# Attention into a feed-forward layer on one core: a planner that counts the early matmuls, the fillers and the V loads differently

## The chip, the core and the metric

The kernel runs on one core of one Trainium2 chip. The metric is device time in microseconds (us) of one execution; lower is better. The engines are TensorE (PE in the profile; PEld is its weight load), VectorE (DVE), ScalarE (ACT), GpSimd (POOL) and SyncE (SP). Each works through its own list of instructions in order and waits on semaphores for the others.

## The reference

Block-causal attention over 8 batches of 8 heads, 576 positions of 64 numbers, in blocks of 64; its output, as 4608 rows of 512, goes through a two-layer network of width 2048.

```python
def _attn_ref(q, k, v):                      # 8, 8, 576, 64
    scores = np.matmul(q, k.transpose(0, 1, 3, 2)) / np.sqrt(D)
    mask = (pos // 64)[:, None] >= (pos // 64)[None, :]
    scores = np.where(mask, scores, -1e9)
    attn = softmax(scores)
    return np.matmul(attn, v)

def _moe_ref(x, w_in, w_out, beta):          # x 4608 x 512, w_in 512 x 2048, w_out 2048 x 512
    h = x @ w_in
    g = h * (1.0 / (1.0 + np.exp(-beta * h)))
    return g @ w_out
```

## The kernel before

Nothing in this kernel is ordered by hand. The program first writes down every piece of work as an `Op` of a class `Plan`: the engines that may do it, how long it holds its engine (`dur`), when its result is there (`lat`), what it depends on, which buffers it takes, a priority, and for a transfer the time that it takes on the queue (`xfer`). `Plan.schedule` then plays all of it through on the host: whenever an engine is free in this play, it takes the op of the lowest priority number whose inputs are there. What comes out of it is one list of ops for each engine. These lists, with the semaphore waits that they need, are the kernel. The planned times themselves do not reach the chip; only the order does, and the count of the fillers described below.

**The work.** A unit is two heads of one batch, so there are 32 units, `u`, four to a batch `b`. For each unit:

- q and k are loaded by SP (L608 for batches 0 and 1, L642 from batch 2 on), cast to bf16 (`QKn`; L615, L653; nearly always on POOL), and turned, so that the head dimension lies on the partitions (`QKT`). In batches 0 and 1 PE turns them (L624) and DVE copies them out (L632); from batch 2 on SP issues a transposing transfer for each pair of units (L660).
- PE multiplies q by k (L692, L436) into PSUM, ACT takes the exponential (L706, L718) into `E`, DVE zeroes the masked corners (L712, L714).
- v is loaded by SP into `Vs` (L538, L541), one such tile for each batch in six transfers, and cast to `Vn` by POOL (L564). In batch 0 the loads for heads 4 to 7 go partly by POOL's queue straight into `Vn`.
- PE multiplies `E` by `Vn` (L744, 30 matmuls of 65 columns), DVE divides by the sum (`inv` L756, `xq` L763). The result is turned into `xT`, by PE for batches 0 to 2 (L783, copied out by L791 and L793), by SP's transposing transfer from batch 3 on (L770).

The network then runs over chunks of 512 rows, `r` from 0 to 8: 16 ops of four matmuls of 512 columns against `w_in` (L967), tanh on ACT (L977), the gate on DVE (L981, `gT`), and the second layer, plain for chunk 0 (L1003), for the others by a seven-product scheme of 2 x 2 blocks (L888) with its sums on DVE (L852, L832). A chunk's first layer needs `xT` of all four units that its rows come from; the weights are loaded by POOL (L492, L497).

**PE's modes.** The q-by-k matmuls use half of the array's rows each (`mode="row"`), everything else the full array (`mode="full"`). The planner adds 140 ns (`SWITCH`) when the mode changes.

**The fillers.** 400 ops of the lowest priority (`NFILL`, priority 1e6 and up) have no result. When PE would be free in the play, before 50 us, it takes a filler: one matmul of 256 columns (L513), or in row mode two of 64 x 64 side by side (L515). Its planned length is 215 ns for the first 12 and 110 ns for all others. A filler that is planned is executed, whether or not PE has time for it on the chip.

**Planned PE lengths** are otherwise fixed: six turning matmuls 258 ns, a q-by-k group 220 or 60 ns, four matmuls of 512 columns 865 ns.

**Planned transfers.** SP's transfers share one ring in the play. A full piece of a V tile has `xfer` 1400 ns in batch 0 and 1580 ns after it; a V tile counts as 4.5 full pieces (four of 128 rows and two of a quarter each). SP's order among loads is fixed (`seq`); the transposing transfers are put between them where the play has them ready.

Of the kernel before, what the change touches and what calls it, by code (L numbers as in the profile page):

```python
# [22 lines left out]
class Tile:  # L23


    def __init__(self, cls):
        self.cls, self.slot, self.left, self.users = cls, None, 0, []
        self.at = (0, 2)
        self.only = None
# [19 lines left out]
class Plan:  # L49
# [9 lines left out]
    BACKLOG = 3000.0  # L59
    RING = 6000.0  # L60
    EARLY = 24000.0

    def __init__(self):
        self.ops = []
# [19 lines left out]
    def schedule(self):  # L84
# [85 lines left out]
        while nsched < len(self.ops) - len(fill) or pend or rings["H"] or rings["S"] or late:  # L170
# [4 lines left out]
            while pend and pend[0][0] <= now + 1e-9:  # L175
                _, _, o = heapq.heappop(pend)
# [20 lines left out]
            while progress:  # L197
                progress = False
                for e in engs:
# [4 lines left out]
                    for o in pool:  # L204
# [7 lines left out]
                        if o.lazy and left["H"] > self.BACKLOG:  # L212
                            continue
                        if o.fill and (now > o.fill or sum(k >= 4 for k in banks) < (3 if now > self.EARLY else 1)):
                            continue
# [16 lines left out]
                    o = best[1]  # L232
# [22 lines left out]
                    start = now  # L255
                    if e == "PE" and mode is not None and o.mode != mode:
                        start += self.SWITCH
                    if e == "PE":
                        mode = o.mode
                    o.eng, o.start, o.end = e, start, start + o.lat  # L260
                    full = 0.0
                    if o.dma is not None:
# [93 lines left out]
def bass_blockwise_causal_attn__then__act_swish_beta_kernel(  # L356
# [10 lines left out]
    with es:  # L367
# [47 lines left out]
        P = Plan()  # L415
# [5 lines left out]
        def mm(n):  # L421
            return max(n / 2.4 + 3, 55.0)
# [8 lines left out]
        def pr(u):  # L431
            b, c = divmod(u, NPAIR)
            return u if b < 1 else 10 * u if b < 2 else 994 + 100 * (b - LAG) + 4.9 * c
# [11 lines left out]
        def mk(fn):  # L445
            return lambda g, e: fn(g)
# [13 lines left out]
        for i in range(NQ):  # L460
# [5 lines left out]
            o = P.op("POOL", 200, mk(lambda g, i=i: g.memset(Vn[i][:, 4, :, 64:66], 0.0)), prio=-5)  # L466
# [6 lines left out]
        for i in range(NQ, NE + 1):  # L473
# [4 lines left out]
                  xfer=100, dma=("d_beta", 1), prio=0.1)  # L478
# [28 lines left out]
        for i in range(NFILL):  # L507
            tf = P.tile("P1")

            def ff(g, e, tf=tf, i=i):  # L510
                o = fills[i]
                if o.mode == "full":
                    return g.matmul(PS[:, tf.slot, 0:256], identB[:], identW)  # L513
                for r in (slice(0, 64), slice(64, 128)):
                    z = g.matmul(PS[r, tf.slot, 0:256], identB[r, r], identW[r, :])  # L515
                return z

            n = 215 if i < 12 else 110
            o = P.op("PE", n, ff, deps=[c2, c4], tiles=[tf], lat=n, mode="full", prio=1e6 + i)
            o.fill = TFILL  # L520
            fills.append(o)
# [4 lines left out]
        for b in range(B):  # L526
            ts, t = P.tile("Vs"), P.tile("V")
            ts.only = (b,) if b < 2 else (0,)
            early += [ts] * (b < 2)
            tl[b] = t  # L530
            for h0, h1, e, tt in PARTS[b]:

                vs = []
                for i in tt:
                    def fv(g, e, ts=ts, t=t, b=b, h0=h0, h1=h1, i=i):
                        d = Vn[t.slot] if e == "POOL" else Vs[ts.slot]
                        if i < 4:
                            return [g.dma_start(d[:, i, h0:h1, 0:64],  # L538
                                                v[b, h0:h1, 128 * i:128 * i + 128, :].rearrange("h p d -> p h d"))]
                        o = i - 4  # L540
                        return [g.dma_start(d[64 * o:64 * o + 64, 4, h0 + o:h1:2, 0:64],  # L541
                                            v[b, h0 + o:h1:2, 512:576, :].rearrange("h p d -> p h d"))]

                    n = (h1 - h0) / 8 * (1 if i < 4 else 0.25)
                    if e == "SP":
                        o = P.op("SP", 300 + 550 * n, fv, tiles=[ts], xfer=(1400 if b == 0 else 1580) * n,
                                 prio=3.5 + 0.1 * (h0 > 0) if b == 0 else 4 * b + (3.5 if b < 2 else 0.5),
                                 dma=["d_V", h0, 1])
                    else:
                        o = P.op("POOL", 150 + 1450 * n, fv, tiles=[t], xfer=1400 * n, prio=-30 if b == 0 else 4 * b + (3.5 if b < 2 else 0.5), dma=["d_VP", h0, 1])  # L550
                        o.after = lastv if b else None
                    vs.append(o)
                ld["V" if e == "SP" else "VP", b, h0] = vs
                if e == "POOL":
                    lastv = vs[-1]
                    for h in range(h0, h1, 2):
                        load.setdefault(4 * b + h // 2, []).extend([*vs, *ones, *vzero])
                    continue
                n = 5 if 4 in tt else len(tt)
                for g0 in range(h0, h1, 2):  # L560
                    g1 = g0 + 2

                    def fw(g, e, ts=ts, t=t, g0=g0, g1=g1, n=n):
                        return g.tensor_copy(Vn[t.slot][:, 0:n, g0:g1, 0:64], Vs[ts.slot][:, 0:n, g0:g1, :])  # L564

                    o = P.op("POOL", 60 + 60 * n * (g1 - g0), fw, deps=[*vs, *ones, *vzero], tiles=[ts, t],
                             prio=4 * b + 0.5 - (38.5 - 5 * (h0 > 0)) * (b < 1))
                    for h in range(g0, g1, 2):
                        load[4 * b + h // 2] = [o]
                lastv = o  # L570
# [12 lines left out]
        def blocks(b):  # L583
            x0 = S * b % RX
            n = min(5, (RX - x0) // 128)
            return [z for z in ((0, n, x0), (n, 5 - n, 0)) if z[1]]
# [4 lines left out]
        for u in range(NU):  # L591
            b, c = divmod(u, NPAIR)
# [7 lines left out]
            if b < QB:  # L600

                turned = []
                for w, (nm, src) in enumerate((("Q", q), ("K", k))):
                    ts, pt = P.tile("ST"), P.tile("P1")
# [6 lines left out]
                    o = ld[nm, u] = P.op("SP", 420, fl, tiles=[ts], xfer=1170, prio=u, dma=["d_S", 0, 1])  # L611
                    o.pkt = 80.0

                    def fn(g, e, ts=ts, tn=tn, p=p, w=w):
# [4 lines left out]
                    o = P.op("POOL" if onp else "DVE", 850 if onp else 750, fn, deps=[o], tiles=[ts, tn],  # L619
                             prio=-40 + 3 * u if onp else -1)  # L620

                    def ft(g, e, tn=tn, pt=pt, p=p, w=w):
                        for i in range(6):
# [4 lines left out]
                    o = P.op("PE", 6 * 43, ft, deps=[o, c4], tiles=[tn, pt, tt_], lat=6 * 43 + 170, mode="full",  # L628
                             prio=pr(u))
# [6 lines left out]
            elif p == 0:  # L636

                for w, (nm, src) in enumerate((("Q", q), ("K", k))):
                    ts = P.tile("S4")

                    def fl(g, e, ts=ts, src=src, b=b, c=c):
# [3 lines left out]
                    o = P.op("SP", QKI, fl, deps=[o for t in early6 for o in t.users] if b == QB else [],  # L645
                             tiles=[ts], xfer=QKX, prio=u, dma=["d_S4", 0, 1])
# [22 lines left out]
            for grp in GROUPS[b]:  # L669
                pst = [P.tile("PP" if g0 < 3 else "P1") for g0 in grp]  # L670

                def fq(g, e, pst=pst, grp=grp, tqk=tqk, p=p, b=b):
                    keep = {}
                    for g0, ps in zip(grp, pst):
# [4 lines left out]
                        for t, q0, q1, off in blocks:  # L679
# [17 lines left out]
                n = sum(220 if g0 < 3 else 60 for g0 in grp)  # L697
                o = P.op("PE", n, fq, deps=cps, tiles=pst + [tqk] + [te] * (b > 0),
                         lat=n + 200, mode="row", prio=pr(u) + .1 + .1*(grp[0] >= 2))
                for g0, ps in zip(grp, pst):  # L700
                    qk[g0] = o, ps
            for g0 in range(4):
                o, ps = qk[g0]
# [64 lines left out]
            if b >= XB:  # L768
# [5 lines left out]
                n = len(blocks(b))  # L774
# [181 lines left out]
        for r in range(NRC):  # L956
# [5 lines left out]
            for j in range(NJ):  # L962
                ph, tt = P.tile("P1"), P.tile("th")

                def fh(g, e, ph=ph, j=j, row=row):
                    for c in range(4):
# [4 lines left out]
                o = P.op("PE", 4 * mm(512), fh, deps=xd + [win[j // 4]], tiles=[ph, tg], lat=4 * mm(512) + 170,  # L971
                         mode="full", prio=1000 + 100 * r + j)
# [21 lines left out]
            for w, d0, d1 in [(w, 0, DM) for w in range(4)]:  # L994
# [4 lines left out]
                o = None  # L999
                for j0, j1 in parts:  # L1000
                    def fo(g, e, po=po, tg=tg, w=w, j0=j0, j1=j1, d0=d0, d1=d1):
                        for j in range(j0, j1):
# [4 lines left out]
                    n = (j1 - j0) * mm(d1 - d0)  # L1007
                    was = o
                    o = P.op("PE", n, fo, deps=gs[j0:j1] + wout[j0 // 4:(j1 + 3) // 4],
                             tiles=[po, tg], lat=n + 170, mode="full",  # L1010
                             prio=1000 + 100 * r + (16 + w + 0.01 * j0 if w == 0 else
                                                     103 + 5.33 * (w - 1) + 1.33 * j0 / 4))
# [84 lines left out]
```

## Time and profile before

| | |
|---|---|
| median of 6 runs | 338.36 us (337.89 to 339.01) |
| the profiled execution, its own time | 337.86 us |
| its span, first to last instruction | 336.0 us |
| busy in the span: PE | 327.2 us (97%) |
| DVE, ACT, POOL | 222.8 (66%), 211.5 (63%), 85.4 us (25%) |
| fillers executed, L513 and L515 | 47 matmuls and 78 matmuls (39 pairs) |
| moved by transfers | 53.41 MB, 159 GB/s over the span |

A PE that is shown as busy is not a PE without gaps: matmuls are pipelined, each is shown with its full passage, and short gaps between starts vanish in it. So the starts of matmuls tell more than their busy time. The chain of waits is followed back from the last instruction, at each step to what released it or, where nothing did, to the instruction before it on its engine.

### The profile page before, as it was taken

To read this page: it belongs to the slowest core of one execution; us is meant where nothing else is said; L and a number is where in the kernel's file an instruction comes from. 1 tells how busy PE (TensorE), PEld (TensorE's weight loads), DVE (VectorE), ACT (ScalarE), POOL (GpSimd) and SP (SyncE) were. 2 spreads that over 40 slices of the span, in tenths; PEclk is the share of its full clock that TensorE was granted. 3 is DMA by queue.
4 is the path that set the end of the run, shared out by engine and by line. 5 is a ranking of instruction groups with operands and counts; after the bars stand their busy time and mean duration, and the time that the engine had idled before them with its cause. 6 is when DMAs were issued, how large, how long until landed. Compare 5 with 4: busy or idle time off the path is not lost.

```text
span 336.0 us, 7537 instructions
## 1 busy us (share of the span) xinstructions
PE 327.2 (97%) x3162; PEld 205.8 (61%) x3106; DVE 222.8 (66%) x449; ACT 211.5 (63%) x314; POOL 85.4 (25%) x127
## 2 busy tenths in 40 slices
PE   7998999999999999999999999999999999999996
PEld 5575445535577556855566666567555766666685
DVE  4638766578763778647956695768376766666742
ACT  1854994188556778659777659775777545545521
POOL 6765081074083025300730342051000000000000
PEclk9999999999999999999999999999999999999999
DMA  7999899999999799999999999997121200020023
GB/s 205 225 246 236 181 213 201 197 288 199 191 247 206 172 215 199 181 172 211 174 172 231 248 196 203 193 173 158 35 54 39 83 32 33 28 68 31 2 95 125
DMA packets 154993, 53.41 MB, mean 159 GB/s; under 512 B 139072, under 2 KB 154448, under 8 KB 154960
## 3 DMA queue, kind: packets, MB, share of 16 engines
q1 hardware_dynamic: 141200, 40.19, 63.3%
q0 software_dynamic: 5568, 4.36, 8.4%
q10 hardware_dynamic: 8192, 8.39, 7.9%
q8 instruction: 24, 0.39, 0.5%
q14 instruction: 9, 0.07, 0.1%
HBM read 36.71 MB, written 9.44 MB: 137 GB/s over the span
## 4 chain that ended last, share of the span: by engine, by line
PE 80%; DVE 6%; DMA 6%; ACT 4%; issue 1%; SPq 1%; POOL 0%; ACTq 0%; POOLq 0%
PE PS L967 31%; PE PS L888 27%; PE PS L744 7%; PE PS L692 7%; PE PS L1003 4%; DMA ST<-in_q_dram 3%; DVE gT L981 3%; ACT E L706 2%; DMA QKT<-QKn 2%; PE PS L515 2%; PE PS L783 1%; ACT th L977 1%; DVE xq L763 1%; PE PS L624 1%; DVE gT L852 1%
## 5 line engine op out<-in xcount | busy, mean ns | idle before, releaser
L967 PE MATMUL PS<-xT,w_in 128*128 128x512 bf16 x576 | 137.5, 380 | 0.7 <-DVE gT L981 0.3
L977 ACT ACTIVATE th<-PS,beta 128x512 f32<-128x512 f32 x144 | 96.7, 697 | 60.0 <-PE PS L967 59.3
L981 DVE SCALAR_TENSOR_TENSOR gT<-th,PS 128x512 f16<-128x512 f32 x144 | 95.8, 683 | 37.0 <-ACT th L977 36.6
L706 ACT ACTIVATE E<-PS 128x1024 bf16<-128x1024 f32 x93 | 92.3, 1029 | 27.3 <-PE PS L692 26.0
L967 PEld LDWEIGHTS PS<-xT,w_in 128*128 128x128 bf16 x576 | 52.7, 98 | 56.9 <-issue 3.6
L888 PE MATMUL PS<-w_out,gT 128*128 128x256 f16 x512 | 63.2, 273 | 0.0
L888 PEld LDWEIGHTS PS<-w_out,gT 128*128 128x128 f16 x512 | 49.0, 98 | 11.3 <-issue 0.2
L653 POOL CAST QKn<-ST 128x640 bf16<-128x640 f32 x48 | 37.8, 788 | 32.0 <-DMA ST<-in_k_dram 16.6
L564 POOL CAST Vn<-Vs 128x640 bf16<-128x640 f32 (+1 forms) x28 | 21.1, 753 | 95.7 <-DMA Vs<-in_v_dram 94.4
L692 PE MATMUL PS<-QKT 64*128 64x192 bf16 (+4 forms) x328 | 37.1, 297 | 0.9 <-DVE xq L763 0.6
L744 PEld LDWEIGHTS PS<-Vn,E 128*128 128x128 bf16 x930 | 31.7, 97 | 3.8 <-DVE xq L763 0.4
L909 ACT ACTIVATE ost<-PS 128x512 f32<-128x512 f32 x32 | 19.2, 599 | 23.5 <-PE PS L888 23.4
L744 PE MATMUL PS<-Vn,E 128*128 128x65 bf16 x930 | 32.8, 193 | 0.3 <-DVE xq L763 0.3
L888 PE MATMUL PS<-OV 128*128 128x256 f16 x256 | 32.0, 273 | 0.0
L692 PEld LDWEIGHTS PS<-QKT 64*128 64x128 bf16 (+1 forms) x328 | 13.4, 95 | 27.6 <-issue 15.9
L888 PEld LDWEIGHTS PS<-OV 128*128 128x128 f16 x256 | 24.3, 98 | 6.1 <-issue 0.4
L763 DVE TENSOR_TENSOR xq<-PS,inv 128x640 bf16<-128x640 f32 x32 | 26.3, 822 | 0.8
L852 DVE TENSOR_TENSOR OV<-gT 128x1024 f16<-128x1024 f16 x32 | 23.8, 756 | 0.5
L712 DVE MEMSET E<- 64x64 uint32 x62 | 6.9, 112 | 23.9 <-ACT E L706 22.1
L912 DVE SCALAR_TENSOR_TENSOR ost<-PS,ost 128x512 f32<-128x512 f32 x22 | 15.0, 681 | 7.7 <-PE PS L888 6.1
L888 PE MATMUL PS<-OV,gT 128*128 128x256 f16 x128 | 16.0, 273 | 0.0
L1003 PE MATMUL PS<-w_out,gT 128*128 128x512 f16 x64 | 15.3, 380 | 0.0
(61 smaller groups left out, 177.8 us busy)
## 6 DMA issues: line engine op xcount, KB each, us to landing
out_dram<-ost ACTq DMA_DIRECT2D x32, 256.0 KB, 3.6
ST<-in_q_dram SPq DMA_DIRECT2D x12, 576.0 KB, 5.5
ST<-in_k_dram SPq DMA_DIRECT2D x12, 576.0 KB, 8.3
Vs<-in_v_dram SPq DMA_DIRECT2D x24, 256.0 KB, 3.9
ST<-in_q_dram SPq DMA_DIRECT2D x8, 288.0 KB, 6.3
ST<-in_k_dram SPq DMA_DIRECT2D x8, 288.0 KB, 7.2
w_in<-in_moe_w_in_dram POOLq DMA_DIRECT2D x4, 512.0 KB, 10.9
w_out<-in_moe_w_out_dram POOLq DMA_DIRECT2D x4, 512.0 KB, 9.3
```

Of the source, the lines that this page charges most:

```text
L564: return g.tensor_copy(Vn[t.slot][:, 0:n, g0:g1, 0:64], Vs[ts.slot][:, 0:n, g0:g1, :])
L653: return g.tensor_copy(QKn[tn.slot][:].rearrange("p a w n -> p (a w n)")[:, 640 * (2 * a + w):][:, 0:640] .rearrange("p (t h d) -> p t h d ...
L692: z = g.matmul(o, QKT[tqk.slot][r, p, 1, 128 * t + y:128 * t + m + y], x)
L706: return g.activation(E3[es_(te)][:, g0, :, :], PS[:, ps.slot:ps.slot + 2, :], ACT.Exp, scale=0.125)
L744: z = g.matmul(o, eblk(te, t, i, h), Vn[Tv.slot][:, t, 2 * c + h, 0:65], start=(t == 0), stop=(t == i))
L763: return g.tensor_tensor(xq[tx.slot][:].rearrange("p i (h d) -> p h i d", h=2), both(pv, 0, 64), x, ALU.mult)
L852: return P.op("DVE", dve_t(SZ * HC / 2), mk(lambda g: g.tensor_tensor(fo(), fx(), fy(), op)), deps=deps, tiles=tiles, prio=prio)
L888: x = g.matmul(PS[:, pw.slot, HM * w:HM * w + HM], fa()[:, j, 128 * w:128 * w + 128], fb()[:, j, :], start=first and (pair or w == 0) and ...
L967: z = g.matmul(PS[:, ph.slot, :], w_in[:, c, 128 * j:128 * j + 128], xT[:, c, row % RX:row % RX + RC], start=(c == 0), stop=(c == 3))
L977: return g.activation(th[tt.slot][:], PS[:, ph.slot, :], ACT.Tanh, scale=beta[:, j:j + 1])
L981: return g.scalar_tensor_tensor(out=gT[tg.slot][:, j, :], in0=th[tt.slot][:], scalar=1.0, in1=PS[:, ph.slot, :], op0=ALU.add, op1=ALU.mult)
L1003: z = g.matmul(PS[:, po.slot, 0:d1 - d0], gT[tg.slot][:, j, 128 * w:128 * w + 128], w_out[:, j, d0:d1], start=(j == 0), stop=(j == NJ - 1))
```

## The change

Three edits, all in what the planner believes; no op is added, no computation changed.

1. A PE op that is planned to start before 7300 ns (`COLD`) counts twice its length, and its result comes later by one length.
2. A filler counts 125 ns, all of them; with the first edit 250 ns before 7300 ns.
3. A full piece of a V tile counts 1400 ns of transfer in every batch.

```diff
@@ class Plan
     EARLY = 24000.0
+    COLD = 7300.0
@@ schedule
                     if e == "PE":
                         mode = o.mode
+                    if e == "PE" and start < self.COLD:
+                        o.lat += o.dur
+                        o.dur *= 2
                     o.eng, o.start, o.end = e, start, start + o.lat
@@ fillers
-            n = 215 if i < 12 else 110
+            n = 125
             o = P.op("PE", n, ff, deps=[c2, c4], tiles=[tf], lat=n, mode="full", prio=1e6 + i)
@@ V loads
                     if e == "SP":
-                        o = P.op("SP", 300 + 550 * n, fv, tiles=[ts], xfer=(1400 if b == 0 else 1580) * n,
+                        o = P.op("SP", 300 + 550 * n, fv, tiles=[ts], xfer=1400 * n,
```

## The prediction

> **What bounds the kernel now.** I read the busy table by windows first. Its columns are busy us of PE, PEld, DVE, ACT and POOL, the granted clock, the share of the transfer engines, and GB/s.
>
> ```profile
> 10.80:21.70 10.90, 10.89 (x149) 6.81 (x150) 5.38 (x16) 9.96 (x15) 6.28 (x9) 1.00 1.26 223
> 21.70:30.50 8.80, 7.35 (x168) 6.20 (x166) 6.86 (x16) 1.86 (x5) 7.56 (x11) 1.00 1.16 242
> 30.50:49.30 18.80, 18.16 (x126) 7.97 (x121) 13.38 (x29) 17.08 (x26) 8.44 (x12) 1.00 1.03 204
> 49.30:235.00 185.70, 184.34 (x1856) 112.68 (x1811) 129.65 (x267) 126.54 (x187) 55.64 (x71) 1.00 1.07 201
> 235.00:320.00 85.00, 85.00 (x683) 54.93 (x674) 56.51 (x99) 50.23 (x75) 0.00 (x0) 1.00 0.15 43
> ```
>
> From 49.3 us on PE has no free time worth the name (184.3 of 185.7, then 85.0 of 85.0), so the end of the run is the moment at which real work begins to flow, plus a fixed amount of work. From 30.5 to 49.3 ACT is the fullest (17.1 of 18.8), fed by the first network matmul at 30.5. A shift of what comes before 30.5 therefore shifts the end, unless a transfer stands in its way. Next, the chain of waits over the head of the run (start, length, what):
>
> ```profile
> 9.93 0.83 POOL QKn L615
> ...
> 10.81 0.43 PE PS L624 x6
> 11.24 0.66 PE PS L513 x6
> ...
> 17.45 0.77 PE PS L515 x12
> 18.23 0.32 PE PS L692 x2
> 18.55 0.99 PE PS L515 x16
> ...
> 21.07 0.66 PE PS L515 x10
> 21.73 1.02 PE PS L744 x30
> ```
>
> Between 10.81 and 21.73 the chain never leaves PE, and half of it is fillers (L513, L515). The first E-by-V product (L744) starts at the instant at which the last fillers end. Was its input there? POOL's timeline answers:
>
> ```profile
> 19.85 1.50 POOL L564 CAST Vn<-Vs 128x640 bf16<-128x640 f32 x2 [4.36 <-DMA Vs<-in_v_dram]
> ```
>
> Two casts in 1.50 us, so the first heads' V is ready at 20.60. PE reached L744 1.1 us after that, because it was executing fillers whose only purpose was to bridge the wait. Last, the cold start on PE's timeline:
>
> ```profile
> 2.38 2.95 PE L513 MATMUL PS<-identF,identB 128*128 128x256 bf16 x13 [2.38 <-POOL identF L449]
> 5.13 0.68 PE L624 MATMUL PS<-identB,QKn 96*128 96x96 bf16 x6
> ...
> 7.00 0.42 PE L624 MATMUL PS<-identB,QKn 96*128 96x96 bf16 x6
> 7.26 1.36 PE L513 MATMUL PS<-identF,identB 128*128 128x256 bf16 x11
> ```
>
> The same matmul starts every 213 ns in the first row (from 2.38 to the next op at 5.13 is 2.75 us for 13, less a short first one) and every 109 ns in the last (1.36 less a passage of 0.27, over 10 steps). The turning matmuls start 80 ns apart in the second row, 42 in the third.
>
> **The change part by part.**
>
> *Cold lengths.* The planner now counts six turning matmuls as 516 ns (chip: 6 x 80 = 480) where it counted 258, and a cold filler as 250 (chip 213) where it counted 215 for twelve and 110 for the rest. Of the 32 fillers that start before the first q-by-k matmul at 8.55 I expect some 22: about 11 before the first turn, 2 and 2 around beta's transpose and the second turn, about 6 after it. The second turn, which started at 7.00 although its cast (5.26 + 0.82) was done at 6.08, can then start near 6.4, and the first q-by-k near 7.9 in place of 8.55. What is this worth at the end? Nothing by itself: the chain passes through the cast at 9.93, which waits for a q load on SP's queue, and the turn at 10.81 starts 0.05 us after that cast. That load covers it; without the cover it would be worth some 0.6 us. Rule and row part here. The Trainium skill, "TensorE: Matmul & The Clock Gate", Part 1, says that the clock is let up to full after some 3.4 us of sustained work, in a free-running window, and that one should not fit to a specific cold count. The trace shows the step from 213 to 109 ns between the matmuls at 5.82 and 6.45, 3.4 to 4.1 us after PE's first. (The granted clock reads 1.00 here and does not show it.) By the row `COLD` is about 1 us too long; by the rule the step moves by half a microsecond from run to run. Either way the sum moves by some 0.5 us x (1 - 109/213), 0.25 us, in a stretch that the cast covers; so zero. The same section speaks against the change in one way: it puts the clock back to half after an idle window of 3.4 us, and fewer fillers leave more idle time. But the planned idle share is only about a tenth, in gaps well below 1 us, and in this trace a PE gap of 0.55 us at 26.88 is followed by matmuls at full rate. I take zero, with 3.4 us x one half = 1.7 us as the far end.
>
> *Fillers at 125.* On the chain from 10.81 to 21.73 lie 10 fillers of L513 (1.10 us together) and 39 of L515 (5.07 us), 6.17 us in all: 126 ns each, where the plan had 110. The planner fills a gap that other engines set (mostly ACT's exponentials), so the planned gap time stays, 49 x 110 = 5.39 us, and now takes 5.39 / 0.125 = 43 fillers. Six fewer, at 126 ns, is 0.74 us less on the chain. The bound above is the V cast: L744 may start at about 20.65 in place of 21.67 to 21.73, so the gain cannot pass 1.05. Below, gaps that happen to round up could leave 0.4. I take 0.7.
>
> Does 0.7 us survive to 30.5? After L744 the chain is PE and DVE alone (L744, `inv`, `xq`, L744, L783, L744, L783), then ACT's `xT` copies and the first L967. The other casts of V (POOL from 22.08, 0.88 us) are done by 22.96, and the third unit's L744 stands at 23.92; it would move to 23.2, still later. The casts of batch 1's q and k run back to back from 24.36, the fourth done at about 27.96, used by the turn at 29.63. Beyond 30.5, two casts wait for loads (31.26 and 34.13, each 0.82 long) and are used at 35.45 and later; `w_in`'s last piece, issued at 23.63 and at most 14.7 us on its way, lands by 38.4 and is used after 43; `w_out`'s last, issued near 47.5 and at most 13.3 on its way, lands by 60.8, near the L1003 at 61.91. That last is the thinnest cover, 1.1 us, and still above 0.7. So all 0.7 arrives.
>
> *V pieces at 1400.* A V tile from batch 1 on counts 4.5 x 180 = 0.81 us less on the planned ring. SP's order of loads is fixed, so what moves is where transposing transfers slip in between, and above all when the planner believes that a batch's later loads, casts and `QKT` are there; PE's list then has that batch's q-by-k earlier among the network's ops. Early batches have room: the transfer issued at 77.81 is landed near 84.9 (median 7.1 us), and its first matmul runs at 89.83. In one place there is none:
>
> ```profile
> 164.61 4.61 DMA ST<-in_q_dram
> 169.22 0.05 issue
> 169.27 0.27 POOL QKn L653
> 169.54 7.56 DMA QKT<-QKn
> 177.10 0.14 issue
> 177.24 0.54 PE PS L692 x6
> ```
>
> This L692 already waits for its transfer (0.18 us on PE). Put 0.81 us earlier in PE's list, it stops PE for up to 0.81. Queued behind it are the L888 ops at 177.71 and 178.60, which need nothing from it. But the load at 164.61 was itself released by an L770 that waited for `xq`, that is by PE; with PE 0.7 earlier it goes 0.7 earlier too. Only the reordering counts, and only if it crosses an op of 0.87 us. Bounds: a gain (attention earlier where ACT is short of work, up to half a microsecond) and 0.8 of loss. No row says which; zero is nearest to a list whose last ops are the same.
>
> Sum: 0 - 0.7 + 0 = -0.7 us. Against the profiled execution, 337.86 (span 336.0 and 1.86 around it), that is 337.16; that execution is 0.5 below the median of the runs shown, so the forecast for the median is 338.36 - 0.7 = 337.7.
>
> **The rivals.** *The head gain arrives (forecast), 0.40:* 337.3 to 338.0, by the bounds 1.05 and 0.4.
>
> *It is eaten, 0.22.* The released PE only waits elsewhere: at the cast of V if that lands later, or behind `w_out`. For it: the transfer share is 1.26 in the very window, and V's cast waited 4.36 us. Against it: that cast's end, 20.60, was 1.1 us ahead of its use. Time 338.4, 338.0 to 338.8.
>
> *PE meets QKT too early, slower, 0.26.* One mechanism: the shorter V makes the planner believe in a second pair of units that has not landed. Its place is the L692 at 177.24 and its like in the batches around. Its price is 0.81 us each time, 1.6 where two V tiles stand ahead of it; two such stops less the head gain, 1.6 + 0.6 - 0.7, give +1.5, time 339.8, and one of them about 339.2. It decides as soon as the stops add to more than 0.7, so from the first stop of full size. For it: the 0.18 us of wait that is there already, and transfer engines at nine tenths through most of the run. Against it: PE-released loads move with PE.
>
> *A better order later, 0.10.* Attention that starts sooner fills stretches in which ACT waits for PE (59.3 us of waits of L977); with the head gain 336.5.
>
> *The clock falls back, 0.02:* +1.0 net, 339.4.
>
> **How the numbers follow.** What a measurement of this kernel can tell from no change is about 0.2%, 0.68 us. Of the forecast's 0.40 I put 0.36 beyond it; with 0.09 of the better order and 0.02 of the second case, faster is 0.47. Slower is 0.24 of the third, 0.02 of the clock, 0.02 of the second: 0.28. The rest, 0.25, is no change. The range 336.1 to 339.7 reaches to the better order below and nearly to two stops above; the likeliest case alone is 337.3 to 338.0.
>
> **What would show it.** Right: about 70 fillers in place of 86; the first L744 near 21.0, with the chain passing to the V cast or just short of it; the first L967 near 29.8; the same lead still there at 49 and at 300. Wrong: L744 at 21.7 again, or early but with L967 at 30.5 (eaten); waits of L692 for QKT of more than half a microsecond at 140 to 235 (third case); filler starts 213 ns apart after 7 us (clock).

## The result, and the profile after

The changed kernel takes 337.21 us (median of 35 runs, 335.88 to 341.72); the kernel before, run beside it, 338.57 (70 runs, 336.84 to 340.96). The ratio is 0.9963, interval 0.995 to 0.9977: 1.25 us faster. The forecast was 0.7 us faster. Six of the 35 executions had a granted clock of 0.99 in place of 1.00; they took 339.03 us (median) where the others took 337.02, and are counted with them. The profiled execution of the changed kernel took 337.56 us (span 335.7), only 0.3 less than that of the kernel before (337.86, span 336.0); this gap between a profile and a median is part of what had to be explained.

The change's first edit added lines, so a line of before is 4 higher here: fillers L517 and L519 (L513 and L515 before), turns L628, q by k L696 and L440, cast of V L568, E by V L748, `xq` L767, `xT` by SP L774, first layer L971, second layer L892. Kernels below without that edit keep the numbers of before.

The busy table by windows, changed kernel, columns as in the prediction:

```profile
10.80:21.70 10.90, 9.81 (x136) 5.81 (x133) 4.66 (x14) 9.48 (x13) 4.54 (x7) 1.00 1.29 219
...
30.50:49.30 18.80, 18.80 (x175) 9.14 (x166) 14.31 (x30) 17.63 (x28) 8.31 (x12) 1.00 1.04 210
...
200.00:240.00 40.00, 39.08 (x381) 24.23 (x369) 25.84 (x53) 28.02 (x42) 5.76 (x8) 1.00 0.79 154
```

In the first row PE is no longer full: 9.81 of 10.90 where it was 10.89, so in this stretch fillers no longer set the pace. In the second, PE and ACT are fuller than before (18.80 and 17.63 where 18.16 and 17.08 stood): the network has work. In the last PE loses 0.92 us of 40 at a place where the kernel before loses none. The chain of waits over the head says what sets the pace now:

```profile
13.44 7.73 DMA Vs<-in_v_dram
21.18 0.05 issue
21.23 0.73 POOL Vn L568
...
22.00 1.02 PE PS L748 x28
```

The first E-by-V product starts when its cast is done, and the cast when the last piece of V that it needs lands, at 21.18. In the profiled execution of before that piece had landed by 19.80. So this execution was ready early and then stood for 1.03 us at a transfer that came 1.4 us later; L748 starts at 22.00, later than L744's 21.67. PE's timeline over the cold start:

```profile
2.38 2.53 PE L517 MATMUL PS<-identF,identB 128*128 128x256 bf16 x11 [2.38 <-POOL identF L453]
4.74 0.66 PE L628 MATMUL PS<-identB,QKn 96*128 96x96 bf16 x6
...
6.17 0.43 PE L628 MATMUL PS<-identB,QKn 96*128 96x96 bf16 x6
...
7.45 0.75 PE L696 MATMUL PS<-QKT 64*128 64x512 bf16 x8
...
10.40 0.43 PE L628 MATMUL PS<-identB,QKn 96*128 96x96 bf16 x6
```

Eleven fillers before the first turn in place of 13, the second turn at 6.17 in place of 7.00, the first q by k at 7.45 in place of 8.55. The fifth turn, from which the prediction counted its fillers (10.81), now stands at 10.40. Counted by their place in PE's list, since the same place comes at another time in each execution, 21 fillers stand ahead of the first q by k where 32 did, 3 where 4 did from there to the fifth turn, and 43 where 49 did from the fifth turn to the first E by V; with 5 later ones (1 before) 72 are executed, against 86.

From there on the two profiled executions compare like this: the first network matmul stands at 31.38 against 30.50, but batch 1's first E by V at 47.73 against 49.12, so by 48 us the changed kernel is 1.4 ahead. Of these, 0.9 is one group of four network matmuls that its list has behind that place. The first L892 is a fairer mark (L888 before; 86.93 against 87.99), since both have then executed the same matmuls but for fillers: there the lead is 1.1. Up to 200 us it is 1.1 to 1.3 wherever the two lists agree, and from 240 us on only 0.3. The lead of about one microsecond is lost between 203 and 206 us, at the place of the last window row.

### The profile page after: what moved, and what is told of

Same layout as the page of the kernel before. It is cut to its first block, busy times and chain, and to the rows that moved or that the text cites. A ratio compares the mean times of both kernels' runs of the same rounds, so it can differ in the third digit from the quotient of the medians.

```text
span 335.7 us, 7500 instructions
## 1 busy us (share of the span) xinstructions
PE 325.5 (97%) x3148; PEld 203.7 (61%) x3092; DVE 220.9 (66%) x449; ACT 211.3 (63%) x314; POOL 84.2 (25%) x127
## 4 chain that ended last, share of the span: by engine, by line
PE 86%; DVE 4%; DMA 4%; ACT 2%; SPq 2%; POOL 0%; issue 0%
PE PS L971 36%; PE PS L892 28%; PE PS L748 8%; PE PS L696 7%; PE PS L1007 4%; DMA Vs<-in_v_dram 2%; ACT E L710 2%; SPq L542 2%; PE PS L787 1%; DMA ST<-in_k_dram 1%; DVE xq L767 1%; DVE gT L985 1%; ACT th L981 1%; PE PS L628 1%; DVE gT L856 1%
## 5 line engine op out<-in xcount | busy, mean ns | idle before, releaser
L971 PE MATMUL PS<-xT,w_in 128*128 128x512 bf16 x576 | 137.3, 380 | 1.0 <-DVE E L718 0.9
L710 ACT ACTIVATE E<-PS 128x1024 bf16<-128x1024 f32 x93 | 91.9, 1025 | 24.1 <-PE PS L696 22.6
L971 PEld LDWEIGHTS PS<-xT,w_in 128*128 128x128 bf16 x576 | 52.6, 98 | 57.0 <-issue 3.4
L892 PE MATMUL PS<-w_out,gT 128*128 128x256 f16 x512 | 63.2, 273 | 0.0
L892 PEld LDWEIGHTS PS<-w_out,gT 128*128 128x128 f16 x512 | 48.8, 98 | 11.7 <-DVE OV L856 0.4
L657 POOL CAST QKn<-ST 128x640 bf16<-128x640 f32 x48 | 37.1, 773 | 31.2 <-DMA ST<-in_k_dram 22.8
L568 POOL CAST Vn<-Vs 128x640 bf16<-128x640 f32 (+1 forms) x28 | 20.9, 746 | 92.3 <-DMA Vs<-in_v_dram 91.0
L696 PE MATMUL PS<-QKT 64*128 64x512 bf16 (+4 forms) x328 | 37.1, 297 | 0.6 <-DVE xq L767 0.3
L748 PEld LDWEIGHTS PS<-Vn,E 128*128 128x128 bf16 x930 | 31.5, 97 | 5.3 <-POOL Vn L568 1.2
L748 PE MATMUL PS<-Vn,E 128*128 128x65 bf16 x930 | 32.9, 193 | 1.5 <-POOL Vn L568 1.0
L892 PE MATMUL PS<-OV 128*128 128x256 f16 x256 | 32.1, 273 | 0.0
L696 PEld LDWEIGHTS PS<-QKT 64*128 64x128 bf16 (+1 forms) x328 | 13.4, 96 | 27.5 <-issue 16.2
L892 PEld LDWEIGHTS PS<-OV 128*128 128x128 f16 x256 | 24.3, 98 | 6.2 <-issue 0.4
L767 DVE TENSOR_TENSOR xq<-PS,inv 128x640 bf16<-128x640 f32 x32 | 26.3, 821 | 0.6
L856 DVE TENSOR_TENSOR OV<-gT 128x1024 f16<-128x1024 f16 x32 | 22.5, 712 | 1.1 <-PE PS L892 0.6
L892 PE MATMUL PS<-OV,gT 128*128 128x256 f16 x128 | 16.0, 273 | 0.0
```

The source lines that it names most:

```text
L657: return g.tensor_copy(QKn[tn.slot][:].rearrange("p a w n -> p (a w n)")[:, 640 * (2 * a + w):][:, 0:640] .rearrange("p (t h d) -> p t h d ...
L696: z = g.matmul(o, QKT[tqk.slot][r, p, 1, 128 * t + y:128 * t + m + y], x)
L710: return g.activation(E3[es_(te)][:, g0, :, :], PS[:, ps.slot:ps.slot + 2, :], ACT.Exp, scale=0.125)
L748: z = g.matmul(o, eblk(te, t, i, h), Vn[Tv.slot][:, t, 2 * c + h, 0:65], start=(t == 0), stop=(t == i))
L767: return g.tensor_tensor(xq[tx.slot][:].rearrange("p i (h d) -> p h i d", h=2), both(pv, 0, 64), x, ALU.mult)
L856: return P.op("DVE", dve_t(SZ * HC / 2), mk(lambda g: g.tensor_tensor(fo(), fx(), fy(), op)), deps=deps, tiles=tiles, prio=prio)
```

## The experiments

All are timed in 5 rounds against the kernel before on the same chip, whose medians were 339.15 (first four), 338.86 (next four) and 338.30 us (last four). In the kernel before, and in e3 and e7, many executions take 2 to 3.6 us longer than the span of their instructions; in all other kernels it is 1.7 to 1.9 us. What lies there stays open. By the medians of the spans alone the gains below would be 0.2 to 0.5 us smaller. Three theories stood first. A: fillers that are executed for real delay the first E by V, and each that is left out is worth about its 126 ns, until V's landing decides. B: the new order of PE's list near 30 us, where batch 1's first q by k stands ahead of the first network matmul, brings the gain. C: the V part carries it.

**Each edit alone, and the two without V**

Cold lengths alone:

```diff
+    COLD = 7300.0
+                    if e == "PE" and start < self.COLD:
+                        o.lat += o.dur
+                        o.dur *= 2
```

> Only the doubled cold lengths; fillers count 215/110 and V 1580 as before. The planned list then has batch 1's first q-by-k group ahead of the first L967, as in the changed kernel, and 12 fillers before 8.5 us in place of 32, but 48 in place of 49 between 10 and 20 us. If the gain comes from the order near 30 us (theory B), -0.8 to -1.4 us against before. If it comes from fewer fillers ahead of the first L744 (theory A, the prediction's), 0 within 0.4. If the V part carries it (theory C), 0.

Measured: 339.97 us, ratio 1.0033 (1.0015 to 1.0051), slower. With fillers left at 215, a cold one counts 430 ns where the chip takes 213, so only 12 are executed up to 8.5 us, where before had 32, and PE stands partly empty. By their lengths, 12 x 0.213 and three turns of 0.48 fill 4.0 of the 6.1 us from 2.38. Its timeline (turns):

```profile
11.02 0.69 PE L628 MATMUL PS<-identB,QKn 96*128 96x96 bf16 x6
...
13.58 0.43 PE L628 MATMUL PS<-identB,QKn 96*128 96x96 bf16 x6
```

A turn takes 0.65 to 0.69 us at half rate and 0.43 at full rate. Here it is still at half rate at 11.02, five microseconds after the changed kernel's turn at 6.17 was at full. L748 starts at 22.95, though V's cast began at 19.70. So this trace puts the loss at the clock, which here comes up late; it is the neighbour of the case to which the prediction gave 0.02 (the clock falls back), and it needs the first edit without the second.

Fillers at 125 alone:

```diff
-            n = 215 if i < 12 else 110
+            n = 125
```

> Only the fillers at 125 ns. 43 fillers in place of 49 between 10 and 20 us; the order near 30 us stays that of before (L967 first). Theory A: -0.5 to -0.9 us. Theory B: 0 within 0.4, since the first L744 then waits for the cast of V where that lands late. Theory C: 0.

Measured: 337.68, ratio 0.9968 (0.9952 to 0.9983). From the fifth turn to the first E by V, 43 fillers are executed in place of 49, exactly the six fewer of the prediction. There are more ahead of the first q by k (39 in place of 32, since a cold filler now counts 125 where it takes 213), and the first turn slips from 5.13 to 6.56. It is faster all the same.

V pieces at 1400 alone:

```diff
-                        xfer=(1400 if b == 0 else 1580) * n,
+                        xfer=1400 * n,
```

> Only the V pieces at 1400 ns. The list up to 30 us is that of before. Theories A and B: a loss of 0 to 1.0 us, because PE's lead of 1.3 us in the profile of the changed kernel shrank to 0.3 between 203 and 212 us. Theory C: -0.5 to -1.2 us.

Measured: 339.84, ratio 1.0039 (1.0015 to 1.0062), slower. Its chain of waits passes through a transposing transfer of `xT`:

```profile
166.67 2.36 DMA xT<-xq
...
169.31 0.81 PE PS L967 x3
```

PE stands 1.08 us there by the record, and another 0.96 us before the first-layer group at 207.71; another `xT` landed at 207.41. Of both groups the trace holds four weight loads but only three matmuls; if the first matmul is missing from the record, the stops are 0.9 and 0.7 us. This profile holds something else too. Its list of PE is that of before up to 30 us, and yet:

```profile
7.65 0.69 PE L624 MATMUL PS<-identB,QKn 96*128 96x96 bf16 x6
...
22.91 1.26 PE L744 MATMUL PS<-Vn,E 128*128 128x65 bf16 x36
```

The turn is still at half rate at 7.65, where before's at 7.00 was at full rate; the first E by V comes 1.24 us later than in the profile of before. The head of this list is not always as fast as that profile showed it.

The change without its V part:

```diff
 (both edits above; V stays)
+    COLD = 7300.0
...
+            n = 125
...
                         xfer=(1400 if b == 0 else 1580) * n,
```

> The change without its V part. Theory A: -0.7. Theory B: -0.8 to -1.4. Both: better than the whole change by up to 1.0 us if the stop near 205 us belongs to the shorter V. Theory C: about 0, so worse than the whole change by 1.

Measured: 337.05, ratio 0.9947 (0.9932 to 0.9963). From the fifth turn to the first E by V it executes 43 fillers, as the changed kernel and e2 do. The timeline, POOL's and PE's rows:

```profile
19.81 1.50 POOL L568 CAST Vn<-Vs 128x640 bf16<-128x640 f32 x2 [4.98 <-DMA Vs<-in_v_dram]
...
20.87 1.98 PE L748 MATMUL PS<-Vn,E 128*128 128x65 bf16 x60
```

With V landed early, the product starts at 20.87, 0.8 earlier than in before's profile and 0.3 after the first of the two casts is done (19.81 + 0.75). So the gain doesn't need V's part, and C falls. In the traces that part has an effect of its own, though. From the first E by V to the first second-layer matmul (L892) all four profiles with all three edits (after and, further below, e8, e9, e11) take 64.92 us, the three without V's part (e4, e10, e12) 65.45 to 66.03; e8 and e10 begin it at nearly the same moment, 21.34 and 21.39, and take 64.92 and 65.45. With the shorter V the planner mixes the next batches' attention and the network's ops differently, and this saves PE at least half a microsecond by 87 us.

**Fillers alone, and the order alone**

From before's finished list the last one (e5) or three (e6) fillers are taken out of each of seven gaps that hold five or more and start between 10 and 19.7 us planned, 7 and 21 in all. Nothing else moves.

```diff
+        gaps = [...]   # runs of fillers in order["PE"], 10000 < start < 19700
+        out_ = {id(o) for g in gaps if len(g) > 4 for o in g[-1:]}   # e6: g[-3:]
+        P.order["PE"] = [o for o in P.order["PE"] if id(o) not in out_]
```

> The list of before with the last filler taken out of each of the seven gaps of five or more fillers that are planned between 10 and 19.7 us (42 left of 49); nothing else moves. Theory A (a filler that is executed delays the first L744 by its own length): 7 x 0.115 to 0.126 us, -0.8 us. If the gain of the 125 ns fillers lay in the order of the ops instead: 0.

> As the run with seven fillers fewer, but three out of each gap, 21 fewer. Theory A with the V cast as its bound: the first L744 at 20.7 to 20.9, -1.0 us by the profile of before and more where PE's clock came up late, so -1.0 to -2.0, not the -2.5 that 21 x 0.12 would give. If the clock falls back for want of fillers: slower by 1 or more, with matmul starts 213 ns apart after 10 us.

Measured: seven fewer 337.71, ratio 0.9961 (0.9945 to 0.9978); 21 fewer 336.86, ratio 0.9936 (0.9918 to 0.9954). At 126 ns, 7 are 0.88 us and 21 are 2.65; the medians moved by 1.15 and 2.00. The second stops short of its sum, and the timeline (POOL's and PE's rows) shows at what:

```profile
20.85 1.51 POOL L564 CAST Vn<-Vs 128x640 bf16<-128x640 f32 x2 [5.91 <-DMA Vs<-in_v_dram]
...
21.63 1.98 PE L744 MATMUL PS<-Vn,E 128*128 128x65 bf16 x60 [1.52 <-POOL Vn L564]
```

PE waits 1.52 us for the cast, and the cast for V, landed at 20.79. This is theory A with its limit. And before's own order near 30 us is kept in both, so B isn't needed.

For B, the one exchange by itself:

```diff
+        # PE: batch 1's first q by k and the first network op change places
+        pe[k], pe[k + 1] = pe[k + 1], pe[k]
```

> The list of before with two ops of PE exchanged near 30 us: the first q-by-k group of batch 1 ahead of the first L967. Nothing else. Theory B (ACT, the fullest engine from 30 to 49 us, gets its first exponential sooner): -0.4 to -0.9 us. Theory A: 0 within 0.3.

Measured: 339.49, ratio 1.001 (0.9988 to 1.0032). B falls: by the interval that exchange gains 0.4 us at most.

**The stop near 205 us**

The timeline of the changed kernel, first rows of SP (the time is that for which the issue holds SP), then of PE:

```profile
195.55 0.58 SPq L542 DMA_DIRECT2D Vs<-in_v_dram  x1
196.17 4.77 SPq L664 DMA_TRANSPOSE QKT<-QKn  x1
200.98 1.96 SPq L774 DMA_TRANSPOSE xT<-xq  x1
...
203.52 1.05 PE L892 MATMUL PS<-OV 128*128 128x256 f16 x8
205.49 1.02 PE L971 MATMUL PS<-xT,w_in 128*128 128x512 bf16 x4 [0.93 <-DVE E L718]
```

This is the last of the four `xT` pieces that the next chunk of 512 rows needs. Before, SP issued it at 193.83 and it landed at 196.48, long before its use at 202.00. With the shorter V tile the planner puts it behind a V load and the `QKT` transfer, which holds SP for 4.77 us: it is issued at 200.98, lands at 205.40, and PE starts the chunk at 205.49. The profile's releaser, a DVE instruction, ended at about the same moment; the landing 0.09 us ahead of the start, and the next experiment, make it the transfer. Exchange the two neighbours on SP:

```diff
+        # SP: d_T (QKT) and the d_TX1_ (xT) planned behind it, near 193 us
+        sp[k], sp[k + 1] = sp[k + 1], sp[k]
```

> The changed kernel with two neighbours on SP exchanged near 196 us: the transposing transfer of xT ahead of that of QKT. If the shorter V costs its time because that xT lands at 205.4 and holds the first L971 of its chunk: xT lands near 201, PE has no stop at 205.5, and the kernel is 0.7 to 1.0 us faster than the changed one, as fast as the change without its V part. If the shorter V loses elsewhere: within 0.3 us of the changed kernel.

Measured: 336.71, ratio 0.9944 (0.992 to 0.9968). To set it beside the changed kernel and the kernel without V's part on one chip, the last four runs were the changed kernel again (e9), without V (e10), this exchange again (e11), and a kernel built on what the others showed (e12).

> The changed kernel itself, beside the two versions of it below on one chip. By the earlier comparison -1.25 us against before.

> The changed kernel with V at 1580 again, the same as the run of the change without its V part. If the shorter V costs about 1 us at one late xT transfer: 0.4 to 1.0 us faster than the changed kernel here. If the difference between the two earlier comparisons was the chip: within 0.3.

> The changed kernel with xT's transfer ahead of QKT's near 196 us, as in the earlier run. If that one place is the price of the shorter V: as fast as the version with V at 1580, within 0.3 us, and 0.4 to 1.0 us faster than the changed kernel.

Measured, in this order: 337.49, 336.69 and 336.00; ratios 0.9973 (0.9953 to 0.9993), 0.9955 (0.9932 to 0.9978), 0.9938 (0.9915 to 0.9962). The changed kernel stops at the same place again (issued 200.53, landed 206.17, L971 at 206.26). With the exchange (e11, the same rows of the timeline):

```profile
195.35 1.74 SPq L774 DMA_TRANSPOSE xT<-xq  x1
197.13 8.22 SPq L664 DMA_TRANSPOSE QKT<-QKn  x2
...
202.78 1.05 PE L892 MATMUL PS<-OV 128*128 128x256 f16 x8
203.66 1.03 PE L971 MATMUL PS<-xT,w_in 128*128 128x512 bf16 x4
```

`xT` lands at 201.58, L971 follows L892 without a gap, and the median is 1.49 us lower than that of the changed kernel (drawing its 22 and 22 executions anew with replacement, 95% of the differences lie between 0.3 and 2.2). So the stop, 1.1 to 1.6 us in the two profiles, is where V's part costs time. Its net effect is smaller, since it also gains the half microsecond above: without V (e10) the median is 0.80 lower than with it (e9), by the same drawing between -0.1 and 1.7, so not clear of zero.

The last kernel is the change without V's part, and two more fillers taken out of each gap, ten in all:

```diff
 (as without V)
+        out_ = {id(o) for g in gaps if len(g) > 4 for o in g[-2:]}
```

> The version with V at 1580 and two more fillers out of each gap of five or more between 10 and 19.7 us, 10 fewer. If fillers still hold the first L744 there where the clock comes up late or V lands early: another 0.2 to 0.6 us, -2.0 to -2.4 against before. If V's landing is the bound in nearly all executions: 0 against the version without this.

Measured: 336.12, ratio 0.9933 (0.9905 to 0.9962). PE now waits for V, with 33 fillers left from the fifth turn to the first E by V:

```profile
20.63 1.98 PE L748 MATMUL PS<-Vn,E 128*128 128x65 bf16 x60 [0.95 <-POOL Vn L568]
```

That is the limit of this head. It and the exchange are the fastest versions seen, not told apart from each other; the exchange is faster than the changed kernel in this comparison, and so is this one (by 1.37 us, 0.4 to 2.4 by the same drawing).

## Why the prediction was right, point by point

*What bounds the head.* Right. Fillers stood on the way to the first E by V; taking only fillers out of before's list makes it faster, in two sizes (e5, e6), and the gain ends where V lands.

*Fillers at 125, six fewer.* Right, to the count: 43 from the fifth turn to the first E by V, in e2 and in the whole change. By its ratio e2 gained 1.08 us (0.6 to 1.6), where six at 126 ns are 0.74.

*The cap of 1.05.* Wrong as a property of the kernel: it was read from one execution in which the head was early. The same opening of before's list stood in five profiles. By the rows of fillers and turns the step from 213 to 109 ns came by 6.3 us in before's profile and, in the others, at times that I work out from those rows as about 6.7 (e6), 7.3 (e5), 7.7 (e7) and 8.4 us (e3). Where also the fillers are before's, the first E by V stood at 21.67, 22.91 (e3) and 23.18 (e7), mean 22.6. In the six profiles with the change's two filler edits (after, e4, e8 to e11) it stood at 22.00, 20.87, 21.34, 22.08, 21.39 and 21.53, mean 21.5. The difference of 1.05 is most of the 1.25 measured, though it sets only three executions against six; the two profiles first compared have the opposite sign. The profiled execution of before was an early one.

*Cold lengths at zero.* This is the term of the sum that was mis-sized. The prediction took them as covered, since the fifth turn started 0.05 us after a cast that waited for its load; without that cover it gave them some 0.6. The cover was there in the one execution that it read. In the other four with the same opening that turn starts 0.6 to 1.3 us after its cast is done, behind delayed turns and fillers, and in e2 1.4. With both filler edits it starts 0.05 to 0.07 after it, in all seven profiles (after, e4, e8 to e12). Rows of the timeline, e3 first, with before's opening, then e4:

```profile
9.53 0.82 POOL L615 CAST QKn<-ST 96x768 bf16<-96x768 f32 x1 [0.35 <-DMA ST<-in_q_dram]
11.64 0.43 PE L624 MATMUL PS<-identB,QKn 96*128 96x96 bf16 x6
...
9.57 0.82 POOL L619 CAST QKn<-ST 96x768 bf16<-96x768 f32 x1 [0.28 <-DMA ST<-in_q_dram]
10.46 0.43 PE L628 MATMUL PS<-identB,QKn 96*128 96x96 bf16 x6
```

What it is worth: with the same 43 fillers behind the fifth turn, e4's median is 0.62 us under that of e2 on the same chip (0.2 to 0.9 by drawing anew), which is the 0.6 of the case without cover. In their profiles the whole difference arises ahead of that turn (10.46 against 11.38); from there to the first E by V both take 10.41 us, and of these 0.9 us half is left at 87 us. Alone the cold lengths lose, by the trace of e1 through the clock.

Two things delay the turn in before's opening. One is the fillers ahead of it: in e2 the rate was full by 6.3 us, and the turn still came 1.4 us behind its cast, with 42 fillers ahead of it where the change has 24. The other is the step to full rate. The Trainium skill, "TensorE: Matmul & The Clock Gate", Part 1, has that step in a free-running window, moving by some 500 ns either way. Here it moved by about 2 us for one and the same opening, more than the page allows. It came by 6.8 us in all seven profiles with both filler edits, and later in three of the five with before's opening; whether the change makes it earlier or seven profiles were lucky was not tried. The prediction took 0.25 us for such a shift and called it covered.

*Does it survive to 30.5?* At 30.5 it doesn't in the two profiles (31.38 against 30.50), because V landed late and a group of q by k was put ahead. By the prediction's own signs this execution would have counted as one in which the gain is eaten: L748 at 22.00, L971 at 31.38, and a lead of only 0.3 at 300. The lead is there at 87 us (1.1), but half a microsecond or more of it is V's part. The signs were set against one early execution; what carries the forecast is e2, e4, e5 and e6, not this profile.

*V at zero.* Its bounds were a gain of up to half a microsecond and a loss of up to 0.8. The traces show both sides: at least half a microsecond gained by 87 us, and 1.1 to 1.6 us lost at one stop near 205; the net measured is a loss of 0.8 that isn't clear of zero (e9 against e10). The slower rival had the right kind of mechanism, a transposing transfer on SP that the planner believes to be there earlier than it is, and its point of decision, one stop of full size against the gain. It named the wrong tile and place: `QKT` at L692 near 177 us, where the changed kernel's chain runs through PE without a wait; the stop is `xT` near 205 us. The prediction said that transposing transfers would slip in elsewhere on SP, but followed this only into PE's list; on SP itself `xT` came to stand behind a `QKT` that holds the queue for 4.8 us.

*Eaten at V's cast.* It happened in the profiled execution (1.03 us) and in e9's (1.50), and the median was still lower. Over the fourteen profiles V's last piece lands between 19.1 and 21.3 us, in the two profiles of the changed kernel at 21.18 and 21.25, the two latest. In e8 and e11, whose lists are those of the changed kernel up to 193 us, it lands at 20.51 and 20.70, so the list alone doesn't make it that late.

So the direction came out by the mechanism that the forecast named. That the size lies near 0.7 (1.25 us, and 0.9 when measured again as e9, interval 0.2 to 1.6) is in part luck: the gain of the head is larger (about 1.8 us in e4, 1.5 in e10, by their ratios), with some 0.6 of it from the cold lengths that stood at zero, and V's part, also at zero, takes some of it back by a stop that was not foreseen.

## What to carry to other kernels

A filler that a planner places is real work: count it at what it takes on the chip, and judge it where the awaited input arrives, over several executions, since the margin read in one profile (1.1 us here from the first V cast's end to its use) was 1.9 in another with the same list up to there (e3: 20.28 + 0.75 to 22.91), and a wait that covers a delay in one execution (the fifth turn, 0.05 us behind its cast) can be gone in the next (1.3 us behind it, e3). Compare two lists by place in the list, not by the clock on the trace. Change the cold length of the real work and of the fillers together; doubling a filler length that was right already left gaps on PE, and the run that did so stayed at half rate past 11 us (e1). When a planned transfer is made shorter, compare the order on the issuing queue before and after, and look for any transfer that moved behind a long one and is needed soon.

## What the runs showed of the hardware that was not expected

- The step to full matmul rate came between about 6 and 8.4 us for one opening of the list, and with 12 fillers before 8.5 us in place of 32 only after the turn at 11.02 (e1: 0.69 us there, 0.43 at 13.58). The granted clock reads 1.00 in every one of these windows and doesn't show it; only the spacing of matmuls does.
- A wait of 1.5 us on PE (e6, e9) did not bring the half rate back: the 60 E-by-V matmuls after it took 1.98 us, as they did without a wait.
- The issue of a transposing transfer holds SP for long: in the changed kernel's profile 4.3 us for `QKT` and 1.25 us for `xT` (medians of 12 and 24), against 0.59 us for a V load (median of 30). Each is at times held much longer (up to 9.8, 4.4 and 4.2 us), so the order on SP matters: the `xT` that was issued behind a `QKT` landed 4 us later than the one issued ahead of it (205.40 in after, 201.58 in e11).
